# Linear attention, 32 heads: the outputs of two neighbouring heads stored by one transfer of 1 MB, and the orders drawn anew

## The chip, the cores and the metric

The kernel runs on one core of a Trainium2 chip. The core has five engines, each with its own in-order list of instructions: TensorE (PE, matmuls and transposes), VectorE (DVE), ScalarE (ACT), GpSimd (POOL) and SyncE (SP, which here only issues DMA transfers). Sixteen DMA engines move the bytes between HBM and the on-chip memory. The metric is the time of one execution in microseconds (us), the median of several runs. A profile shows one execution; its span, from the first to the last instruction, is a little shorter than that execution's time.

## The reference

Batch 1, 32 heads, 2048 positions, head size 128, all in bf16. One head is independent of the others.

```python
B, H, S, D = 1, 32, 2048, 128
phi_q = jnp.where(q > 0, q + 1, jnp.exp(q)) + 1e-6
phi_k = jnp.where(k > 0, k + 1, jnp.exp(k)) + 1e-6
kv = jnp.einsum("bhsd,bhse->bhde", phi_k, v)
z = jnp.einsum("bhsd->bhd", phi_k)
num = jnp.einsum("bhqd,bhde->bhqe", phi_q, kv)
den = jnp.einsum("bhqd,bhd->bhq", phi_q, z)[..., None] + 1e-6
return num / den
```

## The kernel before

**Tiling.** A head's q, k, v and output are 512 KB each. A head lies on the chip as 128 partitions with 16 rows of 128 numbers each (4 KB a partition, `rows`, 16 tiles j). Since max(x, 0) + min(exp(x), 1) is phi without the 1e-6, a head needs two parts of k and two of q: `em` (exp by ACT at L416, then min with 1 and plus 1e-6 by DVE at L392) and `rk` (max with 0, by POOL at L399 or DVE at L398).

**The operations of head h**, by the keys that the orders use:

- `ldk`, `ldv`, `ldq` (L388): loads. q of heads 2 to 29 and k and v of heads 8 to 29 come in pairs of heads, 1 MB each; the others are 512 KB. Each has six slots (`NI`), so a load waits until the users of the head six earlier are done.
- `ek` (L416, ACT), `em` (L392, DVE), `rk` (POOL or DVE, by the table `ON`), `v1` (L429, POOL or DVE): k's two parts, and v copied beside a column of ones, so that the same matmul gives z.
- `kv` (L437, PE): 32 matmuls, accumulated; `kvs` (L403, DVE) copies the result to SBUF. `kv` of the next head waits for it.
- `T` (L455, PE): 16 transposes of q in two halves into one PSUM tile, which must be free of the previous head's `eq`, `rqa` and `rqb`.
- `eq` (L467, ACT), `emq` (L392, DVE), `rqa` (L397, ACT, the first `NA[h]` of 16 tiles) and `rqb` (L398, DVE, the rest): q's two parts.
- `n` (L498, L503, L505, PE): 32 matmuls a head that give numerator and denominator, in two groups (three for head 31), each into PSUM banks that the previous head's division must have left.
- `a`, `r` (L522, L525, DVE), `f` (L529, DVE): 1e-6 added, the reciprocal, and the division into the output tile `o_sb`.
- `st` (L538, SP): the store. `o_sb` has 14 slots (`NO`), so the `f` of head h waits for the store of head h - 14. Heads 2, 3 and 31 are stored in three pieces, some of them for 51, 64, 13, 68 or 60 partitions (`ROWS`, `HALF`); all others with one transfer of 512 KB.
- `w0` to `w9` (L368, PE): 21 warm-up matmuls that use no data.
- `ident`, `ones`, `eps`, `v1ones` (constants), and `exp` (L361), a first activation on `ones` that makes ACT load its table.

**Order.** The table `ORDER` lists, by hand, the keys of each engine in the sequence in which it runs them. `Program.resolve` gives every operation the semaphore waits that its inputs and its slots need; an engine that waits holds up all that stands behind it in its list. SP issues all transfers on one queue, but ldv0.0, which ACT issues on its own (`BY_ACT`); this one load also waits for `ident`.

The loads and stores near each other in SP's list, one line as an example:

```python
        ldv28.0 st11.0 st12.0 ldk30.0 st14.0 ldk31.0 st13.0 ldq30.0 st19.0 ldv30.0 st18.0 st21.0 ldq31.0
```

The start of ACT's list:

```python
        ldv0.0 exp ek0.0 ek0.1 eq0.1 eq0.0 ek1.0 eq1.0 ek2.0 ek3.0 rqa2 eq2.0 ek4.0 eq3.0 rqa3 eq4.0 ek5.0
```

Of the kernel before, what the change touches and what calls it, by code (L numbers as in the profile page):

```python
# [107 lines left out]

ORDER = {
    "PE": """  # L110
        w9 w6 w8 w3 T0.1 T0.0 w1 kv0.0 T1.1 T1.0 kv0.1 w4 w2 kv1.0 w5 w7 w0 T2.1 T2.0 n0.0 kv2.0 n0.1 T3.0
        T3.1 n1.0 n1.1 kv3.0 T4.0 T4.1 n2.0 n2.1 T5.1 T5.0 kv4.0 n3.0 T6.0 T6.1 n3.1 kv5.0 n4.0 T7.1 T7.0
        n4.1 kv6.0 n5.0 T8.0 T8.1 n5.1 kv7.0 n6.0 T9.0 T9.1 kv8.0 n6.1 n7.0 T10.0 T10.1 n7.1 kv9.0 n8.0
        T11.0 n8.1 T11.1 kv10.0 n9.0 T12.0 T12.1 n9.1 kv11.0 n10.0 T13.0 T13.1 n10.1 kv12.0 n11.0 T14.0
        T14.1 n11.1 kv13.0 n12.0 T15.0 T15.1 n12.1 kv14.0 n13.0 T16.0 T16.1 n13.1 kv15.0 n14.0 T17.0 T17.1
        n14.1 kv16.0 n15.0 T18.0 T18.1 n15.1 kv17.0 n16.0 T19.0 T19.1 n16.1 kv18.0 n17.0 T20.0 T20.1 n17.1
        kv19.0 n18.0 T21.1 T21.0 n18.1 kv20.0 n19.0 T22.1 T22.0 n19.1 kv21.0 n20.0 T23.1 T23.0 kv22.0 n20.1
        n21.0 T24.1 T24.0 n21.1 kv23.0 n22.0 T25.1 T25.0 n22.1 kv24.0 n23.0 T26.0 T26.1 n23.1 kv25.0 n24.0
        T27.0 T27.1 n24.1 kv26.0 n25.0 T28.1 T28.0 n25.1 kv27.0 n26.0 T29.0 T29.1 n26.1 kv28.0 n27.0 T30.0
        kv29.0 n27.1 T30.1 n28.0 n28.1 kv30.0 n29.0 T31.0 n29.1 T31.1 kv31.0 n30.0 n30.1 n31.0 n31.1 n31.2  # L120
    """,
    "DVE": """
        ones v1ones0 eps0 rk0.0 v1ones1 em0.0 em0.1 rk0.1 emq0.1 rqb0.1 rqb0.0 v10.1 v11.0 eps1 rk1.0 em1.0
        kvs0 rk2.0 emq0.0 eps2 rqb1.0 rk3.0 emq1.0 kvs1 em2.0 v12.0 r0.0 f0.0 rqb2.0 a0.1 r0.1 kvs2 f0.1
        em3.0 emq2.0 r1.0 em4.0 rqb3.0 emq3.0 a1.1 f1.0 r1.1 f1.1 kvs3 rqb4.0 r2.0 f2.0 em5.0 emq4.0 a2.1
        kvs4 r2.1 rqb5.0 f2.1 r3.0 f3.0 emq5.0 em6.0 a3.1 r3.1 rqb6.0 f3.1 r4.0 kvs5 f4.0 emq6.0 em7.0 a4.1
        r4.1 rqb7.0 f4.1 r5.0 kvs6 f5.0 emq7.0 em8.0 a5.1 r5.1 rqb8.0 f5.1 r6.0 kvs7 f6.0 emq8.0 em9.0 a6.1
        rqb9.0 r6.1 f6.1 r7.0 kvs8 f7.0 emq9.0 em10.0 a7.1 kvs9 r7.1 rqb10.0 f7.1 r8.0 f8.0 emq10.0 em11.0
        a8.1 rqb11.0 r8.1 kvs10 f8.1 r9.0 f9.0 emq11.0 em12.0 a9.1 r9.1 rqb12.0 f9.1 r10.0 kvs11 f10.0
        emq12.0 em13.0 a10.1 r10.1 rqb13.0 f10.1 r11.0 kvs12 f11.0 emq13.0 em14.0 a11.1 r11.1 rqb14.0 f11.1  # L130
        r12.0 kvs13 f12.0 emq14.0 em15.0 a12.1 r12.1 rqb15.0 f12.1 r13.0 kvs14 f13.0 emq15.0 em16.0 a13.1
# [6 lines left out]
        kvs25 r23.1 rqb26.0 f23.1 r24.0 f24.0 em27.0 emq26.0 a24.1 kvs26 r24.1 rqb27.0 f24.1 r25.0 f25.0  # L138
        emq27.0 em28.0 a25.1 kvs27 r25.1 rqb28.0 f25.1 r26.0 f26.0 em29.0 emq28.0 a26.1 r26.1 kvs28 f26.1
        rqb29.0 r27.0 emq29.0 f27.0 a27.1 r27.1 kvs29 f27.1 em30.0 r28.0 f28.0 a28.1 r28.1 kvs30 f28.1  # L140
        em31.0 r29.0 f29.0 emq30.0 emq31.0 kvs31 a29.1 emq31.1 r29.1 emq31.2 f29.1 r30.0 f30.0 a30.1 r30.1
        f30.1 r31.0 f31.0 a31.1 r31.2 r31.1 f31.2 f31.1
    """,
    "ACT": """
        ldv0.0 exp ek0.0 ek0.1 eq0.1 eq0.0 ek1.0 eq1.0 ek2.0 ek3.0 rqa2 eq2.0 ek4.0 eq3.0 rqa3 eq4.0 ek5.0
        eq5.0 rqa5 ek6.0 eq6.0 rqa6 ek7.0 eq7.0 rqa7 ek8.0 eq8.0 rqa8 ek9.0 eq9.0 rqa9 ek10.0 eq10.0 rqa10
# [8 lines left out]
        rk10.0 v110.0 v111.0 rk11.0 v112.0 rk12.0 v113.0 rk13.0 v114.0 rk14.0 v115.0 rk15.0 v116.0 rk16.0
        rk17.0 v117.0 rk18.0 v118.0 v119.0 rk19.0 v120.0 rk20.0 rk21.0 v121.0 v122.0 rk22.0 rk23.0 v123.0
        rk24.0 v124.0 v125.0 rk25.0 v126.0 rk26.0 rk27.0 v127.0 v128.0 rk28.0 rk29.0 v129.0 rk30.0 v130.0
        rk31.0 v131.0
# [12 lines left out]

# [95 lines left out]
def bass_standalone__linear_attn_elu__prompt_kernel(nc: bass.Bass, q: bass.AP, k: bass.AP, v: bass.AP, out: bass.AP):  # L267
    B, H, S, D = q.shape
    assert D == P and S == 16 * P and B * H == NH
    NT = S // P  # L270
# [5 lines left out]
    qf, kf, vf, of = (t.rearrange("b h s d -> (b h) s d") for t in (q, k, v, out))  # L276
    rows = lambda t, h: t[h].rearrange("(p j) d -> p j d", j=NT)

    with ExitStack() as es:
# [85 lines left out]
        def warm(key, n):  # L365
            def g(e):
                for w in range(n):
                    ins = e.matmul(o_ps[:, 512:992], lhsT=ident[:], rhs=_ap(ident[:, :], 0, [[0, 4], [1, 120]]),  # L368
                                   start=(w == 0), stop=(w == n - 1))
# [215 lines left out]
```

## Time and profile before

| what | value |
|---|---|
| median of 3 runs | 167.99 us (167.9 to 168.12) |
| the profiled execution's own time | 167.83 us |
| its span | 166.5 us |
| PE busy | 156.6 us (94%), 2709 matmuls |
| DVE busy | 154.6 us (93%), 307 instructions |
| ACT busy | 146.6 us (88%) |
| POOL busy | 83.7 us (50%) |
| TensorE clock granted | 0.994 |
| HBM | 50.33 MB read, 16.78 MB written, 403 GB/s over the span |
| stores of 512 KB | 29, median 15.5 us from issue to landing |
| paired loads of 1 MB | q 14 (17.6 us), k 11 (16.4 us), v 11 (15.0 us) |

How to read it: the profile gives for each engine the time in which it ran instructions. Waiting and the issuing of DMA transfers aren't busy time. "q" behind an engine's name is its sequencer, which issues the transfers. A transfer's time to landing includes the wait behind the transfers that were issued earlier. The profile names tiles `la` throughout, so that instructions are told apart by line, shape and place in time; in each engine's list they run in the order of `ORDER`.

### The profile page before, as it was taken

The numbers are of one execution on the slowest core, as the hardware profiler recorded it, in microseconds if no ns is written. First come the engines' busy times: TensorE is split into PE (matmuls) and PEld (weight loads), VectorE is DVE, ScalarE is ACT, GpSimd is POOL, SyncE is SP. The second block draws the span as 40 slices with busy tenths as digits, with TensorE's granted clock in tenths as the row PEclk, the third lists the DMA queues.
The fourth block names the chain that finished last, engine by engine and source line by source line (L and its number), as shares of the span: only waits on it lengthen the run. The fifth ranks groups of instructions, "written<-read, shape, count | busy, mean of one in ns | idle before, by whom it ended". The sixth has DMA issues, their size and how long they took to land.

```text
span 166.5 us, 6111 instructions
## 1 busy us (share of the span) xinstructions
PE 156.6 (94%) x2709; PEld 150.9 (91%) x2709; DVE 154.6 (93%) x307; ACT 146.6 (88%) x99; POOL 83.7 (50%) x64
## 2 busy tenths in 40 slices
PE   4999997999999999999999999999999999999950
...
DVE  0498999999999999999999999999999999999992
...
DMA  5999999999999999999999999999999999999997
GB/s 224 410 424 411 422 403 418 403 405 404 420 418 412 414 406 427 411 423 410 417 408 423 415 424 404 420 415 424 407 416 422 413 416 414 416 416 413 385 396 279
DMA packets 16542, 67.51 MB, mean 405 GB/s; under 512 B 1539, under 2 KB 1923, under 8 KB 14723
## 3 DMA queue, kind: packets, MB, share of 16 engines
q1 hardware_dynamic: 16371, 66.59, 98.5%
q8 instruction: 21, 0.34, 0.8%
q10 hardware_dynamic: 144, 0.52, 0.8%
...
HBM read 50.33 MB, written 16.78 MB: 403 GB/s over the span
## 4 chain that ended last, share of the span: by engine, by line
PE 83%; DMA 7%; DVE 6%; SPq 2%; issue 0%
PE la L437 33%; PE la L503 18%; PE la L505 16%; PE la L455 16%; DMA la<-in_q_dram 7%; DVE la L529 4%; SPq L388 2%; DVE la L398 1%; DVE la L525 1%; PE la L498 0%; DVE la L522 0%; DVE la L403 0%
## 5 line engine op out<-in xcount | busy, mean ns | idle before, releaser
L529 DVE TENSOR_TENSOR la<-la 128x1536 bf16<-128x1536 f32 (+1 forms) x65 | 77.9, 1200 | 0.6
L503 PE MATMUL la<-la 128*128 128x129 bf16 x512 | 66.6, 219 | 0.1
L505 PE MATMUL la<-la 128*128 128x129 bf16 x512 | 66.6, 219 | 0.0
L399 POOL TENSOR_SCALAR la<-la 128x2048 bf16<-128x2048 bf16 x28 | 53.0, 1893 | 26.2 <-DVE la L522 18.7
L467 ACT ACTIVATE la<-la 128x2048 bf16<-128x2048 bf16 (+2 forms) x35 | 60.2, 1728 | 5.0 <-PE la L455 3.1
L416 ACT ACTIVATE la<-la 128x2048 bf16<-128x2048 bf16 (+1 forms) x33 | 61.3, 1865 | 3.4 <-DMA la<-in_k_dram 1.9
L437 PE MATMUL la<-la 128*128 128x129 bf16 x1024 | 63.4, 220 | 0.0
L437 PEld LDWEIGHTS la<-la 128*128 128x128 bf16 x1024 | 59.3, 98 | 0.8 <-DVE la L403 0.4
L429 POOL COPY la<-la 128x1024 int32<-128x1024 int32 (+1 forms) x30 | 31.2, 1043 | 41.1 <-PE la L437 22.7
L505 PEld LDWEIGHTS la<-la 128*128 128x128 bf16 x512 | 49.8, 97 | 0.0
L503 PEld LDWEIGHTS la<-la 128*128 128x128 bf16 x512 | 48.1, 97 | 0.3 <-DVE la L529 0.2
L392 DVE TENSOR_SCALAR la<-la 128x2048 bf16<-128x2048 bf16 (+2 forms) x68 | 42.4, 658 | 1.1 <-ACT la L416 1.1
L455 PE MATMUL la<-la 128*128 128x128 bf16 x512 | 35.3, 222 | 1.0 <-DMA la<-in_q_dram 0.9
L455 PEld LDWEIGHTS la<-la 128*128 128x128 bf16 x512 | 30.7, 99 | 2.7 <-DMA la<-in_q_dram 1.5
L397 ACT ACTIVATE la<-la 128x1024 bf16<-128x1024 bf16 (+2 forms) x29 | 31.6, 1091 | 0.0
L398 DVE TENSOR_SCALAR la<-la 128x1024 bf16<-128x1024 bf16 (+2 forms) x36 | 24.4, 682 | 4.7 <-DMA la<-in_k_dram 4.6
L498 PE MATMUL la<-la 128*128 128x3 bf16 (+1 forms) x128 | 21.6, 168 | 2.5 <-DVE la L529 2.5
L498 PEld LDWEIGHTS la<-la 128*128 128x128 bf16 x128 | 12.5, 98 | 2.8 <-DVE la L529 2.8
L525 DVE RECIPROCAL la<-la 128x12 f32<-128x12 f32 (+1 forms) x65 | 12.9, 200 | 1.0 <-PE la L505 0.2
L403 DVE CAST la<-la 128x129 bf16<-128x129 f32 x32 | 8.3, 258 | 0.0
L368 PE MATMUL la<-la 128*128 128x480 bf16 x21 | 6.7, 468 | 1.5 <-POOL la L353 1.5
L368 PEld LDWEIGHTS la<-la 128*128 128x128 bf16 x21 | 2.3, 120 | 3.9 <-issue 1.7
(15 smaller groups left out, 9.7 us busy)
## 6 DMA issues: line engine op xcount, KB each, us to landing
out_dram<-la SPq DMA_DIRECT2D x29, 512.0 KB, 15.5
la<-in_q_dram SPq DMA_DIRECT2D x14, 1024.0 KB, 17.6
la<-in_v_dram SPq DMA_DIRECT2D x11, 1024.0 KB, 15.0
la<-in_k_dram SPq DMA_DIRECT2D x11, 1024.0 KB, 16.4
...
```

The source lines that it names most:

```text
L392: add(on(key, "DVE"), key, lambda e: e.tensor_scalar(t, t, 1.0, EPS, op0=ALU.min, op1=ALU.add), deps)
L397: "ACT": lambda e: e.activation(dst, src, ACT.Relu),
L399: "POOL": lambda e: e.tensor_scalar(dst, src, BIG, 0.0, op0=ALU.min, op1=ALU.max)}[eng], deps)
L416: add("ACT", key, lambda e, a=a, b=b: e.activation(em_sb[:, h % NE, a:b], k_sb[:, h % NI["k"], a:b], ACT.Exp), [f"ldk{k0}.0"] + fill("em", ...
L429: add(on(key, "POOL"), key, lambda e, a=a, b=b, word=word: e.tensor_copy(v1_sb[:, h % NV, a:b, 0:D].bitcast(word), v_sb[:, h % NI["v"], a: ...
L437: ins = e.matmul(kv_ps, lhsT=src[:, j], rhs=v1_sb[:, h % NV, j, 0:NC], start=(j + part == 0), stop=(j == NT - 1 and part == 1))
L455: ins = e.transpose(to, src, ident[:])
L467: add("ACT", key, lambda e, a=a, b=b: e.activation(part(emq_sb, a, b), src(a, b), ACT.Exp), over("T", h, t_parts, a, b) + fill("emq", NQ, ...
L498: e.matmul(_ap(o_ps[:, :], o + D, [[NC, m]]), lhsT=ones[:], rhs=epsr[:, 0:m], start=True, stop=False, skip_group_check=True)
L503: e.matmul(to, lhsT=tile(emq_sb, t), rhs=kvs_sb[:, h % NK, 0:NC], start=late and c == 0, stop=False, skip_group_check=True)
L505: ins = e.matmul(to, lhsT=tile(rq_sb, t), rhs=kvs_sb[:, h % NK, 0:NC], start=False, stop=True, skip_group_check=True)
L529: return e.tensor_tensor(out=_ap(o_sb[:, :, :, :], first(o_sb[:, h % NO, t0, 0:1]) - first(o_sb[:, :, :, :]), [[m * D, nb], [D, m], [1, D] ...
```

## The change

The stores of heads 4 to 27 are joined in twelve pairs. One transfer of 1 MB moves both heads of a pair; each partition's 8 KB in `o_sb` go out as 4 KB of the first head and 4 KB of the second. It waits for both heads' divisions, has one semaphore, and frees both slots. Heads 0 to 3 and 28 to 31 are stored as before. SP's list has 85 transfers instead of 97.

All five lists of `ORDER` were drawn anew. Among what differs besides the stores' places:

- ACT runs `exp` before it issues `ldv0.0`, and `eq2.0` before `rqa2`.
- `v10.0` and `v13.0` move from POOL to DVE; `v10.1`, `rk0.0` and `rk2.0` from DVE to POOL. `v10.0` is DVE's third operation.
- PE's warm-up matmuls stand elsewhere; `w2` (4 matmuls) now comes between `kv1.0` and `T2`.
- ACT takes 14 instead of 8 tiles of q's relu in head 28 (`NA`).
- Many loads and stores have other places in SP's list.

```diff
-ON = {"rk0.1": "DVE", "v10.1": "DVE", "rk0.0": "DVE", "rk1.0": "DVE", "rk2.0": "DVE", "rk3.0": "DVE", "v12.0":
-      "DVE", "v11.0": "DVE"}
+ON = {"rk0.1": "DVE", "v11.0": "DVE", "rk1.0": "DVE", "rk3.0": "DVE", "v12.0": "DVE", "v10.0": "DVE", "v13.0":
+      "DVE"}
+SFIRST, SLAST = 4, 28
...
+def spair(h):
+    return SFIRST <= h < SLAST
...
-NA = (8, 0, 10, 8, 0, 8, 8, 8, 8, 8, 8, 8, 8, 8, 8, 8, 8, 8, 8, 8, 8, 8, 8, 8, 8, 8, 8, 8, 8, 8, 16, 16)
+NA = (8, 0, 10, 8, 0, 8, 8, 8, 8, 8, 8, 8, 8, 8, 8, 8, 8, 8, 8, 8, 8, 8, 8, 8, 8, 8, 8, 8, 14, 16, 16, 16)
...
     "PE": """
-        w9 w6 w8 w3 T0.1 T0.0 w1 kv0.0 T1.1 T1.0 kv0.1 w4 w2 kv1.0 w5 w7 w0 T2.1 T2.0 n0.0 kv2.0 n0.1 T3.0
-        T3.1 n1.0 n1.1 kv3.0 T4.0 T4.1 n2.0 n2.1 T5.1 T5.0 kv4.0 n3.0 T6.0 T6.1 n3.1 kv5.0 n4.0 T7.1 T7.0
+        w5 w8 w6 w7 T0.0 T0.1 w1 kv0.0 T1.0 T1.1 w3 w4 kv0.1 w9 w0 kv1.0 w2 T2.1 T2.0 n0.0 kv2.0 n0.1 T3.0
+        T3.1 n1.0 n1.1 kv3.0 T4.1 T4.0 n2.0 n2.1 T5.0 T5.1 kv4.0 n3.0 T6.1 T6.0 n3.1 kv5.0 n4.0 T7.1 T7.0
...
-        T27.0 T27.1 n24.1 kv26.0 n25.0 T28.1 T28.0 n25.1 kv27.0 n26.0 T29.0 T29.1 n26.1 kv28.0 n27.0 T30.0
-        kv29.0 n27.1 T30.1 n28.0 n28.1 kv30.0 n29.0 T31.0 n29.1 T31.1 kv31.0 n30.0 n30.1 n31.0 n31.1 n31.2
+        T27.0 T27.1 n24.1 kv26.0 n25.0 T28.0 T28.1 n25.1 kv27.0 n26.0 n26.1 T29.0 T29.1 kv28.0 n27.0 kv29.0
+        n27.1 T30.1 T30.0 n28.0 kv30.0 n28.1 n29.0 T31.0 T31.1 n29.1 kv31.0 n30.0 n30.1 n31.0 n31.1 n31.2
     "DVE": """
-        ones v1ones0 eps0 rk0.0 v1ones1 em0.0 em0.1 rk0.1 emq0.1 rqb0.1 rqb0.0 v10.1 v11.0 eps1 rk1.0 em1.0
-        kvs0 rk2.0 emq0.0 eps2 rqb1.0 rk3.0 emq1.0 kvs1 em2.0 v12.0 r0.0 f0.0 rqb2.0 a0.1 r0.1 kvs2 f0.1
-        em3.0 emq2.0 r1.0 em4.0 rqb3.0 emq3.0 a1.1 f1.0 r1.1 f1.1 kvs3 rqb4.0 r2.0 f2.0 em5.0 emq4.0 a2.1
+        ones eps0 v10.0 v1ones0 em0.1 em0.0 rk0.1 rqb0.0 rqb0.1 emq0.0 eps2 rk1.0 emq0.1 em1.0 v11.0 v1ones1
+        kvs0 rqb1.0 emq1.0 eps1 em2.0 kvs1 rk3.0 v12.0 em3.0 r0.0 f0.0 rqb2.0 kvs2 a0.1 r0.1 f0.1 v13.0
+        em4.0 emq2.0 r1.0 rqb3.0 emq3.0 a1.1 f1.0 r1.1 f1.1 kvs3 rqb4.0 r2.0 emq4.0 f2.0 em5.0 a2.1 kvs4
...
     "ACT": """
-        ldv0.0 exp ek0.0 ek0.1 eq0.1 eq0.0 ek1.0 eq1.0 ek2.0 ek3.0 rqa2 eq2.0 ek4.0 eq3.0 rqa3 eq4.0 ek5.0
+        exp ldv0.0 ek0.1 ek0.0 eq0.0 eq0.1 ek1.0 eq1.0 ek2.0 ek3.0 eq2.0 rqa2 ek4.0 eq3.0 rqa3 eq4.0 ek5.0
...
     "POOL": """
-        ident0 ident v10.0 v13.0 rk5.0 rk4.0 v14.0 v15.0 v16.0 rk6.0 rk7.0 v17.0 rk8.0 v18.0 v19.0 rk9.0
+        ident0 ident rk0.0 v10.1 rk2.0 rk4.0 rk5.0 v14.0 v15.0 v16.0 rk6.0 rk7.0 v17.0 rk8.0 v18.0 v19.0
...
     "SP": """
-        ldq0.0 ldk0.0 ldq1.0 ldk1.0 ldv1.0 ldk3.0 ldk2.0 ldq2.0 ldv2.0 ldk4.0 ldv3.0 ldk5.0 ldq4.0 ldv5.0
-        ldv4.0 ldv6.0 ldk6.0 ldq6.0 ldv8.0 ldk7.0 ldv7.0 ldk8.0 ldq8.0 st0.0 ldv10.0 st3.1 ldk10.0 ldq10.0
-        ldv12.0 ldk12.0 ldq12.0 ldv14.0 st1.0 st3.2 ldk14.0 ldq14.0 st2.2 ldv16.0 st2.1 ldk16.0 ldq16.0
-        st2.0 st4.0 ldv18.0 ldk18.0 ldq18.0 ldv20.0 st3.0 ldk20.0 ldq20.0 st5.0 st7.0 ldk22.0 ldq22.0
-        ldv22.0 st6.0 ldv24.0 ldq24.0 ldk24.0 st8.0 ldq26.0 st9.0 ldv26.0 ldk26.0 st10.0 ldk28.0 ldq28.0
-        ldv28.0 st11.0 st12.0 ldk30.0 st14.0 ldk31.0 st13.0 ldq30.0 st19.0 ldv30.0 st18.0 st21.0 ldq31.0
-        ldv31.0 st15.0 st24.0 st17.0 st16.0 st20.0 st25.0 st23.0 st22.0 st27.0 st28.0 st29.0 st26.0 st30.0
-        st31.0 st31.2 st31.1
+        ldq0.0 ldk0.0 ldq1.0 ldk1.0 ldv1.0 ldk2.0 ldk3.0 ldq2.0 ldv2.0 ldk4.0 ldv3.0 ldk5.0 ldq4.0 ldv4.0
+        ldv5.0 ldq6.0 ldv6.0 ldk6.0 ldv8.0 ldk7.0 ldv7.0 ldk8.0 ldq8.0 ldq10.0 ldk10.0 st2.1 ldv10.0 ldv12.0
+        ldq12.0 ldk12.0 ldq14.0 st3.0 ldk14.0 st1.0 st3.2 st0.0 ldv14.0 ldk16.0 st3.1 ldv16.0 ldq16.0
+        ldv18.0 ldq18.0 ldk18.0 st2.2 ldv20.0 ldq20.0 st2.0 st7.0 ldk20.0 st5.0 ldk22.0 ldv22.0 ldq22.0
+        ldv24.0 ldq24.0 ldk24.0 st9.0 ldq26.0 ldv26.0 ldk26.0 st11.0 ldv28.0 ldk28.0 ldq28.0 st13.0 ldq30.0
+        ldv31.0 ldk31.0 ldv30.0 ldk30.0 st15.0 st23.0 ldq31.0 st17.0 st19.0 st27.0 st21.0 st25.0 st29.0
+        st28.0 st30.0 st31.0 st31.2 st31.1
...
+            if spair(h):
+                if h % 2:
+                    key = f"st{h}.0"
+                    add("SP", key, lambda e: e.dma_start(of[h - 1:h + 1].rearrange("h (p j) d -> p h j d", j=NT),
+                                                         o_sb[:, (h - 1) % NO:(h - 1) % NO + 2]),
+                        [f"f{x}.{j}" for x in (h - 1, h) for j in range(len(groups(x)))], dma=f"o{(h - 1) % NO}")
+                    used("o", NO, (h - 1, h), key)
+                return
             for i, (a, b, x, y) in enumerate(st_parts(h)):
```

More of the change, by code (lines that the diff above doesn't have):

```diff
@@ L110 @@
     "PE": """
-        w9 w6 w8 w3 T0.1 T0.0 w1 kv0.0 T1.1 T1.0 kv0.1 w4 w2 kv1.0 w5 w7 w0 T2.1 T2.0 n0.0 kv2.0 n0.1 T3.0
-        T3.1 n1.0 n1.1 kv3.0 T4.0 T4.1 n2.0 n2.1 T5.1 T5.0 kv4.0 n3.0 T6.0 T6.1 n3.1 kv5.0 n4.0 T7.1 T7.0
-        n4.1 kv6.0 n5.0 T8.0 T8.1 n5.1 kv7.0 n6.0 T9.0 T9.1 kv8.0 n6.1 n7.0 T10.0 T10.1 n7.1 kv9.0 n8.0
-        T11.0 n8.1 T11.1 kv10.0 n9.0 T12.0 T12.1 n9.1 kv11.0 n10.0 T13.0 T13.1 n10.1 kv12.0 n11.0 T14.0
+        w5 w8 w6 w7 T0.0 T0.1 w1 kv0.0 T1.0 T1.1 w3 w4 kv0.1 w9 w0 kv1.0 w2 T2.1 T2.0 n0.0 kv2.0 n0.1 T3.0
+        T3.1 n1.0 n1.1 kv3.0 T4.1 T4.0 n2.0 n2.1 T5.0 T5.1 kv4.0 n3.0 T6.1 T6.0 n3.1 kv5.0 n4.0 T7.1 T7.0
+        n4.1 kv6.0 n5.0 T8.1 T8.0 n5.1 kv7.0 n6.0 T9.0 T9.1 n6.1 kv8.0 n7.0 T10.0 T10.1 n7.1 kv9.0 n8.0
+        T11.0 T11.1 n8.1 kv10.0 n9.0 T12.0 T12.1 n9.1 kv11.0 n10.0 T13.0 T13.1 n10.1 kv12.0 n11.0 T14.0
         T14.1 n11.1 kv13.0 n12.0 T15.0 T15.1 n12.1 kv14.0 n13.0 T16.0 T16.1 n13.1 kv15.0 n14.0 T17.0 T17.1
@@ L137 @@
         f21.1 r22.0 f22.0 em25.0 emq24.0 a22.1 rqb25.0 r22.1 f22.1 r23.0 kvs24 f23.0 emq25.0 em26.0 a23.1
[L138 to L142, printed above, removed]
+        kvs25 r23.1 rqb26.0 f23.1 r24.0 f24.0 emq26.0 em27.0 a24.1 rqb27.0 r24.1 kvs26 f24.1 r25.0 f25.0
+        emq27.0 em28.0 a25.1 r25.1 kvs27 f25.1 r26.0 rqb28.0 f26.0 emq28.0 em29.0 a26.1 kvs28 r26.1 f26.1
+        r27.0 f27.0 emq29.0 a27.1 kvs29 r27.1 f27.1 em30.0 r28.0 f28.0 a28.1 kvs30 r28.1 f28.1 emq30.0 r29.0
+        em31.0 f29.0 emq31.2 emq31.1 a29.1 emq31.0 r29.1 f29.1 kvs31 r30.0 f30.0 a30.1 r30.1 f30.1 r31.0
+        f31.0 a31.1 r31.2 r31.1 f31.2 f31.1
     """,
     "ACT": """
-        ldv0.0 exp ek0.0 ek0.1 eq0.1 eq0.0 ek1.0 eq1.0 ek2.0 ek3.0 rqa2 eq2.0 ek4.0 eq3.0 rqa3 eq4.0 ek5.0
+        exp ldv0.0 ek0.1 ek0.0 eq0.0 eq0.1 ek1.0 eq1.0 ek2.0 ek3.0 eq2.0 rqa2 ek4.0 eq3.0 rqa3 eq4.0 ek5.0
         eq5.0 rqa5 ek6.0 eq6.0 rqa6 ek7.0 eq7.0 rqa7 ek8.0 eq8.0 rqa8 ek9.0 eq9.0 rqa9 ek10.0 eq10.0 rqa10
@@ L149 @@
         ek21.0 eq21.0 rqa21 ek22.0 eq22.0 rqa22 ek23.0 eq23.0 rqa23 ek24.0 eq24.0 rqa24 ek25.0 eq25.0 rqa25
-        ek26.0 eq26.0 rqa26 ek27.0 eq27.0 rqa27 ek28.0 eq28.0 rqa28 ek29.0 eq29.0 rqa29 ek30.0 ek31.0 eq30.0
-        rqa30 eq31.0 eq31.2 eq31.1 rqa31
+        ek26.0 eq26.0 rqa26 ek27.0 eq27.0 rqa27 ek28.0 rqa28 eq28.0 ek29.0 eq29.0 rqa29 ek30.0 eq30.0 rqa30
+        ek31.0 eq31.0 eq31.1 eq31.2 rqa31
     """,
     "POOL": """
-        ident0 ident v10.0 v13.0 rk5.0 rk4.0 v14.0 v15.0 v16.0 rk6.0 rk7.0 v17.0 rk8.0 v18.0 v19.0 rk9.0
@@ L155 @@
[L155 to L158, printed above, removed]
+        ident0 ident rk0.0 v10.1 rk2.0 rk4.0 rk5.0 v14.0 v15.0 v16.0 rk6.0 rk7.0 v17.0 rk8.0 v18.0 v19.0
+        rk9.0 rk10.0 v110.0 v111.0 rk11.0 v112.0 rk12.0 v113.0 rk13.0 v114.0 rk14.0 v115.0 rk15.0 v116.0
```

9 lines of the change are left out of this document (6 added, 3 removed).

## The prediction

> **What bounds the kernel now.** I read the page's slices, then windows by engine, then the start of each engine's timeline, the chain of waits, the tail, and last the DMA issues one by one. First two rows of the slices and the DMA rows:
>
> ```profile
> PE   4999997999999999999999999999999999999950
> DVE  0498999999999999999999999999999999999992
> DMA  5999999999999999999999999999999999999997
> q1 hardware_dynamic: 16371, 66.59, 98.5%
> ```
>
> Three things are full at once. The windows of all engines say how full (columns: stretch, its length, then busy us of PE, PEld, DVE, ACT, POOL, clock, DMA share and GB/s):
>
> ```profile
> 60.00:90.00 30.00, 30.00 (x550) 30.00 (x548) 29.76 (x60) 29.62 (x20) 19.48 (x14) 1.00 1.02 415
> 156.00:158.00 2.00, 1.94 (x34) 1.63 (x31) 1.93 (x8) 0.99 (x1) 0.00 (x0) 1.00 0.84 342
> 158.00:164.00 6.00, 2.13 (x37) 1.92 (x36) 5.27 (x11) 0.00 (x0) 0.00 (x0) 1.00 0.98 394
> 164.00:166.50 2.50, 0.00 (x0) 0.00 (x0) 0.00 (x0) 0.00 (x0) 0.00 (x0) 0.64 0.57 213
> ```
>
> From 30 to 158 us PE never stops, one head each 4.62 us, and the DMA engines never stop either. So there are two ends: the chain of PE and DVE (last division f31.1 over at 163.38) and the DMA queue (last landing 166.48). The order of everything between decides neither as long as both stay fed. Only the start, where PE still idles, and the tail can move. The start is in the timelines (start, length, instruction, idle before it and its releaser):
>
> ```profile
> 1.50 0.41 ACTq L388 DMA_DIRECT2D la<-in_v_dram  x1
> 1.94 1.28 ACT L361 ACT_TABLE_LOAD   x1 [1.94 <-POOL la L353]
> 3.23 0.21 ACT L361 ACTIVATE la<-la 128x1 bf16<-128x1 bf16 x1
> ...
> 5.17 0.43 DVE L398 TENSOR_SCALAR la<-la 128x1024 bf16<-128x1024 bf16 x1 [4.12 <-DMA la<-in_k_dram]
> ...
> 7.11 0.61 POOL L429 COPY la<-la 128x512 int32<-128x512 int32 x1 [5.65 <-DMA la<-in_v_dram]
> ```
> ```profile
> 12.44 1.99 PE L437 MATMUL la<-la 128*128 128x129 bf16 x32
> 14.26 0.97 PE L368 MATMUL la<-la 128*128 128x480 bf16 x4
> 15.43 1.05 PE L455 MATMUL la<-la 128*128 128x128 bf16 x16 [0.19 <-DMA la<-in_q_dram]
> ```
>
> ldv0 is issued at 1.50, before the table load and exp, and lands at 7.06; POOL copies it while DVE already works from 5.17. PE has warm-up matmuls (L368) to spare until ldq2 lands at 15.29. Then the chain of waits has, in the window from 24 us:
>
> ```profile
> 25.15 1.66 DVE la L529
> ...
> 27.82 1.20 DVE la L398
> ...
> 29.07 1.07 PE la L455 x16
> ```
>
> f1.0 holds n2.0 (1.03 us of PE idle), then rqb4 holds T5 until 29.07. From T5 on PE runs without a gap, so whatever T5 loses, the compute end loses.
>
> **The change, part by part.** Base: span 166.5, profiled execution 167.83, that is 1.33 around the span; the median 167.99 is 0.16 above that execution.
>
> 1. *Twelve pair stores for 24 single ones.* Bytes, queue and packet size (4 KB) stay. Landings one after another price the two forms: the 13 half-megabyte transfers from the landing of st12 (135.26) to that of st24 (151.50) take 16.24, 1.249 each; the 10 stores from there to st26 (163.91) take 1.241 each. The trace has no paired store; the nearest rows are the paired k and v loads, the same pattern the other way: ldv8, ldk8, ldv12, ldk12 land 2.53, 2.55, 2.56, 2.54 after the one ahead, against 2 x 1.277 for single loads at 24 to 29 us. Bounds for the twelve: from 12 x (2.53 - 2.555) = -0.3 to +0.9, if a paired store moved at the single loads' 1.277 rather than 1.241 (24 halves x 0.036). I take 0, nearest to loads that show no difference. Each transfer also ends in a 4-byte packet of 9 ns on each DMA engine: -0.1. [...]
>
> By the Trainium skill, DMA: Bandwidth & Descriptors, section "Rules for kernel authors", a transfer should have 1 MiB or more, and its section "Anatomy of one DMA" gives 2.0 us fixed per transfer; twelve fewer would be 24 us less, 144. The landings 1.25 apart say that this part is hidden behind the next transfer, so the sum goes by the rows.
>
> 2. *The SP queue drawn anew.* Counted in half megabytes, I moved each load's measured landing by 1.26 per unit that its place moved and compared with its first use. All stay in time; the closest are ldv14 (6.0 later, 0.2 to spare), ldk30 (5.0 later, 0.3), ldq22 (3.0 later, 4.25 shrinks to 0.5), ldk20 (3.0 later, 0.7) and ldq28 (3.0 later, 0.9). Slots of o: st15 now frees slots 0 and 1 at about 145.3 for f28.0 at 149.29; the others have 3.7 or more. SP's longest block is at st27, for f27.1 at 148.3: what was queued before it lands until 152.9, 4.6 of cover, of which an issue needs about 1.0 (first packet 1.77 after an issue at 0.73). Behind it wait st21, st25, st29, st28, st30, st31, which hold up only the end itself. Cost 0; without that cover, the excess one to one.
>
> 3. *Start.* ACT issues ldv0 after exp. exp waits only for `ones` (over at 0.99); with 1.28 and 0.21 the issue comes at 2.48 rather than 1.50. At the measured 5.6 to landing it lands at L = 8.1; bounds 7.1 (if the engines reach it as soon as before) and 9.1 (one more queued transfer first). DVE now begins with v10.0, so DVE starts at L instead of 5.17, but gives rk0.0 (0.43), v10.1 (0.41) and rk2.0 (0.69) to POOL, which is idle until 20.5, and takes v10.0 (0.41) and v13.0 (0.69). Walked with the measured steps from one DVE instruction to the next: v10.0 0.38, em0.1 and em0.0 0.35 each, rk0.1 0.34, rqb0.0 and rqb0.1 0.60 each, emq0.0 0.38, rk1.0 0.60, emq0.1 0.34, em1.0 0.60, v11.0 0.62: kvs0 starts at L+5.2 and ends at L+5.5 (12.38 before). PE: kv1.0 at L+5.5, 1.82 long, then w2 with four warm-up matmuls (0.8): T2 at L+8.1 = 16.2 against 15.43. n0.0 then ends at L+10.6, f0.0 at L+12.65, rqb2.0 at L+13.15, so T3 at L+13.2 = 21.3 (20.16). ACT runs eq2.0 ahead of rqa2, then ek4.0, eq3.0, rqa3: eq4 ends at L+20.9, since T4 waits behind kv3.0 (over at L+17.85). rqb4.0 (1.23) follows, T5 at L+22.15 = 30.25: **+1.2** (bounds +0.4 at 7.1, where ldq2's landing binds, +2.2 at 9.1).
>
> 4. *Head 28.* ACT relu 14 tiles instead of 8: (1.237 - 1.025) / 2 = 0.106 a tile, +0.64, covered by ACT's gaps of 1.09 and 1.12 before ek31.0 and eq31.0; DVE -0.45, not on the path, since f30.0 waits for n30.0 (157.36). T29 stands behind n26.1 now (140.0 for 139.57), and rqb28, which now waits for rqa28 too, ends near 139.9. Cost 0; without those gaps 0.2 to 0.6.
>
> 5. *Tail.* The last store is issued when f31.1 ends. Before: 163.40, landed 166.48, 3.08 later. On an empty queue the first load took 2.70 to 3.19 from issue to its first and last landing, 1.27 of it data; with the store's 8 packets of 65 ns (0.52) that is 1.95 to 2.44. So 0.64 to 1.13 of compute delay hides behind the stores queued ahead; I take 0.8.
>
> **Sum:** 1.2 - 0.8 = +0.4 on the compute end; the DMA end alone would be -0.1. Span 166.9, median about 168.4.
>
> **Rivals.** *B, the cover is enough:* ldv0 lands near 7.1, T5 loses 0.4, and the queue alone sets the end: 167.99 - 0.1 = 167.9. For it: both ends are full and the bytes equal; before, ldv0's packets began only at 4.45, behind two loads, so a later issue may cost little. Against: DVE's first work hangs on ldv0 now. Decides if T5 is less than 0.6 to 1.1 late.
>
> *C, faster:* the seams between stores cost DMA time. With -0.3 and -0.1 from part 1 and B's start, 167.5. For it: single loads lost 0.02 per megabyte to paired ones. Against: stores already run at 1.241.
>
> *D, slower by loads:* the queue is late where slack shrank, above all ldq22, on which PE itself waits. Beyond 0.5 plus whatever PE is already late (so from about 1.7 at +1.2) each us is a us. A queue 2.5 late gives +0.8 on A: 169.2. For it: the landings drift by 3 us against a straight line over the run, since some DMA engines run behind others, by up to 4.8. Against: the measured landings already hold that lag.
>
> *E, paired stores are slow:* the halves of a partition's 8 KB lie 512 KB apart in HBM, so the writes lose what part 1's upper bound says, all on the DMA end: +0.9 - 0.1 = 168.8. Against: paired loads with that distance show nothing. The Trainium skill, DMA: Bandwidth & Descriptors, "Latency and other measured facts", has copies with a pitch of 512 KiB between partitions at 207 GB/s against 214; that is the rule that speaks against the change, no row here shows it for writes, and 3% of the paired stores' 30 us would be 1.0.
>
> That the store isn't what it says (fewer engines, smaller packets) has under 1 in 100: the paired loads do it.
>
> **Chances.** A 0.38, B 0.25, C 0.17, D 0.14, E 0.06. A change within 0.2% (0.34 us) can't be told from none here. A's own range is 168.1 to 169.0; 0.10 of it lies under 168.33, 0.28 above; 0.04 of B lies below 167.65. Faster 0.17 + 0.04 = 0.21, same 0.10 + 0.21 = 0.31, slower 0.28 + 0.14 + 0.06 = 0.48. The range: C with some margin at 167.3, D and the upper bound of part 3 (+2.2 - 0.8) at 169.5.
>
> **What would show it.** ldv0's issue near 2.5 and DVE's first copy near 8.1; T2 near 16.2, T5 near 30.2, n30.0 over near 158.5; no PE gap after T5; twelve 1 MB stores landing 2.5 after the one ahead; DMA share 1.02 to 158. T5 before 29.5 makes B or C right; a PE gap at L455 after 30 us, D; stores 2.55 or more apart, E.

## The result and the profile after

| | before | after |
|---|---|---|
| median of 10 runs each | 168.00 us (167.75 to 168.15) | 168.71 us (168.18 to 170.11) |
| ratio, 95% interval | | 1.0045 [1.0028, 1.0062] |
| the profiled execution's own time | 167.83 | 168.68 |
| its span | 166.5 | 167.4 |
| T2, T3, T5 start | 15.43, 20.16, 29.07 | 16.43, 21.05, 29.99 |
| n30.0 over, f31.1 over | 157.36, 163.38 | 158.36, 164.38 |
| last four landings | 166.42, 166.45, 166.46, 166.48 | 166.45, 166.51, 166.60, 167.34 |

The changed kernel is 0.45% slower, 0.7 us. Starts, ends and landings are read from the trace of one execution each. "n30.0 over" is the end of head 30's first group of `n`, "f31.1 over" that of the last division; a store lands sixteen times, once on each DMA engine, and the last four of these landings are given. The rows of the page after that answer to those of before, slices and DMA queues (packets, MB, share of 16 engines):

```profile
PE   4989997999999999999999999999999999999950
DVE  0199899999999999999999999999999999999992
DMA  5999999999999999999999999999999999999995
q1 hardware_dynamic: 16179, 66.59, 98.0%
q8 instruction: 21, 0.34, 0.8%
...
q14 instruction: 6, 0.05, 0.1%
...
out_dram<-la SPq DMA_DIRECT2D x12, 1024.0 KB, 17.2
```

The bytes are the same, twelve stores carry 1 MB. The `instruction` rows count the packets that bring the engines their instructions. They stand on the page of before too; the prediction passed them over. Windows of all engines after (columns as before):

```profile
60.00:90.00 30.00, 30.00 (x550) 30.00 (x548) 29.76 (x61) 29.48 (x21) 19.10 (x13) 1.00 1.02 414
156.00:158.00 2.00, 2.00 (x41) 2.00 (x39) 1.84 (x7) 2.00 (x2) 0.00 (x0) 1.00 1.00 408
158.00:164.00 6.00, 3.08 (x50) 2.55 (x48) 5.86 (x14) 0.00 (x0) 0.00 (x0) 1.00 0.96 386
164.00:166.50 2.50, 0.00 (x0) 0.00 (x0) 0.38 (x1) 0.00 (x0) 0.00 (x0) 0.66 0.66 243
```

In the middle nothing changed: PE full, DMA share 1.02. From 158 to 164 PE has 3.08 us of work left where it had 2.13: compute comes about 1 us later into the tail. Where it lost that is seen in the timelines of ACT, DVE (one row) and PE (start, length, instruction, idle before it):

```profile
0.73 1.28 ACT L365 ACT_TABLE_LOAD   x1 [0.73 <-PEq L582]
1.50 0.41 ACTq L392 DMA_DIRECT2D la<-in_v_dram  x1
2.03 0.20 ACT L365 ACTIVATE la<-la 128x1 bf16<-128x1 bf16 x1
```
```profile
7.77 0.43 DVE L433 COPY la<-la 128x1024 bf16<-128x1024 bf16 x1 [6.75 <-DMA la<-in_v_dram]
```
```profile
13.79 1.99 PE L441 MATMUL la<-la 128*128 128x129 bf16 x32 [0.39 <-DVE la L407]
15.62 0.97 PE L372 MATMUL la<-la 128*128 128x480 bf16 x4
16.43 1.06 PE L459 MATMUL la<-la 128*128 128x128 bf16 x16
```

ldv0 is issued at 1.50 as before, not at 2.5: the table load starts at 0.73, and the issue goes out beside it, ahead of the ACTIVATE that stands in front of it in the list. DVE waits 6.75 us for this load, which lands at 7.74 (7.06 before, from the same issue), and then everything follows from it: kv1 at 13.79, the four warm-up matmuls of `w2`, T2 at 16.43. The chain of waits, window from 24 us:

```profile
26.07 1.67 DVE la L533
...
28.75 1.20 DVE la L402
...
29.99 1.01 PE la L459 x15
```

The same three links as before (f1.0, rqb4, T5), 0.92 later. From there PE has no gap of its own but those of the tail, which were there before, so f31.1 is 1.00 later. Yet all landings but one are over at 166.60, 0.12 later than before. That one comes alone at 167.34, and it ends the run.

### The profile page after: what moved, and what is told of

Its sections match the earlier page's. It is cut to its first block, busy times and chain, and to the rows that moved or that the text cites. A ratio compares the mean times of both kernels' runs of the same rounds, so it can differ in the third digit from the quotient of the medians.

```text
span 167.4 us, 6085 instructions
## 1 busy us (share of the span) xinstructions
PE 156.5 (94%) x2709; PEld 150.9 (90%) x2709; DVE 153.6 (92%) x305; ACT 148.1 (88%) x99; POOL 86.3 (52%) x65
## 4 chain that ended last, share of the span: by engine, by line
PE 83%; DVE 10%; DMA 4%; ACT 0%; issue 0%
PE la L441 34%; PE la L507 17%; PE la L509 16%; PE la L459 16%; DVE la L533 5%; DMA la<-in_v_dram 4%; DVE la L402 2%; DVE la L396 2%; DVE la L433 1%; DVE la L529 1%; PE la L372 0%; ACT L365 0%; DVE la L407 0%; PE la L502 0%; DVE la L526 0%
## 5 line engine op out<-in xcount | busy, mean ns | idle before, releaser
L403 POOL TENSOR_SCALAR la<-la 128x2048 bf16<-128x2048 bf16 (+1 forms) x30 | 56.4, 1879 | 38.3 <-DVE la L526 16.8
L441 PEld LDWEIGHTS la<-la 128*128 128x128 bf16 x1024 | 59.3, 98 | 2.4 <-DVE la L396 1.3
L509 PEld LDWEIGHTS la<-la 128*128 128x128 bf16 x512 | 49.8, 97 | 0.0
L507 PEld LDWEIGHTS la<-la 128*128 128x128 bf16 x512 | 48.1, 97 | 0.4 <-DVE la L407 0.3
L433 POOL COPY la<-la 128x1024 int32<-128x1024 int32 (+1 forms) x29 | 30.4, 1051 | 27.2 <-PE la L441 25.7
L401 ACT ACTIVATE la<-la 128x1024 bf16<-128x1024 bf16 (+3 forms) x29 | 33.2, 1144 | 0.2 <-PE la L509 0.2
L459 PEld LDWEIGHTS la<-la 128*128 128x128 bf16 x512 | 30.6, 99 | 2.2 <-DMA la<-in_q_dram 1.5
L402 DVE TENSOR_SCALAR la<-la 128x1024 bf16<-128x1024 bf16 (+3 forms) x33 | 22.2, 678 | 0.0
L502 PEld LDWEIGHTS la<-la 128*128 128x128 bf16 x128 | 12.5, 98 | 2.7 <-DVE la L533 2.7
L433 DVE COPY la<-la 128x2048 bf16<-128x2048 bf16 (+1 forms) x4 | 2.5, 622 | 6.8 <-DMA la<-in_v_dram 6.8
```

The costliest lines, as they stand in the source:

```text
L401: "ACT": lambda e: e.activation(dst, src, ACT.Relu),
L403: "POOL": lambda e: e.tensor_scalar(dst, src, BIG, 0.0, op0=ALU.min, op1=ALU.max)}[eng], deps)
L433: add(on(key, "POOL"), key, lambda e, a=a, b=b, word=word: e.tensor_copy(v1_sb[:, h % NV, a:b, 0:D].bitcast(word), v_sb[:, h % NI["v"], a: ...
L441: ins = e.matmul(kv_ps, lhsT=src[:, j], rhs=v1_sb[:, h % NV, j, 0:NC], start=(j + part == 0), stop=(j == NT - 1 and part == 1))
L459: ins = e.transpose(to, src, ident[:])
L502: e.matmul(_ap(o_ps[:, :], o + D, [[NC, m]]), lhsT=ones[:], rhs=epsr[:, 0:m], start=True, stop=False, skip_group_check=True)
```

## The experiments

All ratios are against the kernel before, run on the same chip among the others. Three groups were run; in them the kernel before had medians of 168.13 (35 runs), 168.19 (27) and 168.14 (34). "f31.1" is the end of the last division, "others" the last landing but one, "packet" the start of the last 8 KB `instruction` packet, all from the one execution that was profiled, which need not be the median one: that of `pairs` is its longest of eleven (168.33), that of `early` its longest of twelve (169.32), that of `single` one of its long ones (168.86).

| kernel | ratio [95%] | T5 | f31.1 | others | last landing | packet |
|---|---|---|---|---|---|---|
| before | | 29.07 | 163.38 | 166.46 | 166.48 | 160.9 |
| after | 1.0045 [1.0028, 1.0062] | 29.99 | 164.38 | 166.60 | 167.34 | 165.9 |
| pairs | 0.9997 [0.9988, 1.0007] | 30.44 | 164.72 | 166.69 | 166.91 | 162.0 |
| newstart | 0.9998 [0.9989, 1.0007] | 29.91 | 164.17 | 166.65 | 166.66 | 160.8 |
| single | 1.0018 [1.0000, 1.0036] | 30.50 | 165.08 | 167.06 | 167.52 | 164.4 |
| oldstart | 1.0026 [1.0010, 1.0042] | 30.24 | 164.65 | 166.81 | 166.87 | 162.4 |
| oldstart_sp | 0.9999 [0.9990, 1.0007] | 29.43 | 164.20 | 166.77 | 166.85 | 162.3 |
| less_before | 0.9938 [0.9925, 0.9950] | 29.60 | 163.89 | 165.86 | 165.87 | 160.4 |
| less_after | 1.0022 [1.0013, 1.0031] | 29.87 | 164.24 | 166.21 | 167.17 | 165.8 |
| pad | 1.0035 [1.0018, 1.0051] | 29.63 | 164.00 | 166.94 | 167.14 | 165.8 |
| dvepad | 1.0022 [1.0005, 1.0038] | 29.79 | 164.20 | 166.79 | 166.98 | 162.1 |
| tail | 1.0033 [1.0023, 1.0044] | 29.98 | 164.38 | 166.93 | 167.30 | 166.0 |
| early | 1.0012 [1.0000, 1.0023] | 30.66 | 165.05 | 167.02 | 167.98 | 166.6 |
| both | 1.0012 [0.9999, 1.0024] | 29.68 | 164.09 | 166.79 | 166.84 | 162.0 |

**The pair stores alone** (`pairs`): the kernel before, with the paired store and each pair at a place near those of its two singles.

```diff
+SFIRST, SLAST = 4, 28
...
-        ldv28.0 st11.0 st12.0 ldk30.0 st14.0 ldk31.0 st13.0 ldq30.0 st19.0 ldv30.0 st18.0 st21.0 ldq31.0
...
+        ldk24.0 ldq26.0 st9.0 ldv26.0 ldk26.0 ldk28.0 st11.0 ldq28.0 ldv28.0 st13.0 ldk30.0 st15.0 ldk31.0
+        ldq30.0 ldv30.0 st19.0 st21.0 ldq31.0 ldv31.0 st17.0 st25.0 st23.0 st27.0 st28.0 st29.0 st30.0 st31.0
```

> The kernel before with nothing changed but the stores of heads 4 to 27, joined in twelve pairs, each at a place in SP's list where its slots are freed in time and no load comes more than two half megabytes later. Theory S: the pairs cost nothing, 167.8 to 168.2, twelve landings 2.5 us after the one ahead. Rival P: 168.5 to 168.9, steps over 2.55. Rival F: depends on where the instruction packets of SP's shorter list fall; 168.5 if one falls after 164 us, else 168.0.

168.03 against 168.13: no difference. The other way round (`single`), the changed kernel with its pairs taken apart at the same places:

```diff
-SFIRST, SLAST = 4, 28
+SFIRST, SLAST = 32, 32
...
-        ldv31.0 ldk31.0 ldv30.0 ldk30.0 st15.0 st23.0 ldq31.0 st17.0 st19.0 st27.0 st21.0 st25.0 st29.0
...
+        ldq30.0 ldv31.0 ldk31.0 ldv30.0 ldk30.0 st14.0 st15.0 st22.0 st23.0 ldq31.0 st16.0 st17.0 st18.0 st19.0
+        st26.0 st27.0 st20.0 st21.0 st24.0 st25.0 st29.0 st28.0 st30.0 st31.0 st31.2 st31.1
```

> The changed kernel with each paired store split into two single ones at the same place; all orders kept. Theory S: stays at 168.6 to 168.8, T5 near 30.0. Rival P (pairing itself costs): 168.0 to 168.2. Rival F: SP's list is as long as before's again, so its last instruction packet falls earlier, and the time is 168.0 to 168.3 although T5 stays at 30.0.

168.36: 1.0018, with an interval that begins at 1.0000, so slower than before by little or nothing, and if anything less slow than the changed kernel; the intervals overlap. `pairs` is the clear one of the two: pairing brings nothing and of itself costs nothing.

**The start alone** (`newstart`, the kernel before with the changed start) and the reverse (`oldstart`, the changed kernel with the old start):

`newstart` takes `ON` and the beginnings of the five lists from the changed kernel (PE to n3.0, DVE to kvs4, ACT to ek5.0, POOL to v14.0, SP to ldk5.0), `oldstart` takes the same from the kernel before. ACT's first line of the two:

```python
        exp ldv0.0 ek0.1 ek0.0 eq0.0 eq0.1 ek1.0 eq1.0 ek2.0 ek3.0 eq2.0 rqa2 ek4.0 eq3.0 rqa3 eq4.0 ek5.0 eq5.0
        ...
        ldv0.0 exp ek0.0 ek0.1 eq0.1 eq0.0 ek1.0 eq1.0 ek2.0 ek3.0 rqa2 eq2.0 ek4.0 eq3.0 rqa3 eq4.0 ek5.0 eq5.0
```

> The kernel before with the changed start alone: ON and the lists of all engines up to head 4 as changed; single stores and before's order after that. Theory S (the start costs the difference of the changed kernel and oldstart, 0.19%): 168.3 to 168.6, T2 at 16.1 or later in its profile. Rival B (the DMA queue alone sets the end, so the start is free): 168.0 to 168.2.

> The changed kernel with the start of before: the table ON of before and the lists of PE, DVE, ACT, POOL and SP in before's order up to head 4, all later orders and the paired stores kept. Theory S (the start sets the end: T5 0.92 us later, f31.1 1.0 later): T5 back at 29.1, f31.1 back at about 163.4, median 168.0 to 168.2, 0.0 to +0.1% against before. Rival P (the paired stores or the new queue order cost): stays at 168.6 to 168.9. Rival F (the 8 KB instruction packet at 165.92 on one DMA engine makes most of the loss, since SP's list is the same as in the changed kernel): 168.4 to 168.7, with one landing 0.5 or more behind the rest.

`newstart` loses what was forecast for the compute and ends at the same time: T5 at 29.91, f31.1 0.79 later, 168.10 against 168.19. Its windows:

```profile
158.00:164.00 6.00, 2.87 (x47) 2.37 (x44) 5.83 (x13) 0.00 (x0) 0.00 (x0) 1.00 0.97 388
164.00:166.50 2.50, 0.00 (x0) 0.00 (x0) 0.17 (x1) 0.00 (x0) 0.00 (x0) 1.00 0.65 245
```

PE has 2.87 us left after 158 (2.13 before), but the DMA share is 0.97 and 0.65 (0.98 and 0.57 before): the queue still sets the end. `oldstart`, with the start taken back, stays slow at 168.58. So the start alone doesn't make a kernel slow, and taking it back doesn't make the changed one fast.

One thing came out otherwise than expected: in the profile of `oldstart` T5 isn't back at 29.1 but at 30.24, later than in the changed kernel, and in `pairs`, also with the old start, it is at 30.44. There DVE's third copy of v, v12.0, waits for its load, and PE's `kv2` behind it (first row `oldstart`, second `pairs`):

```profile
18.30 0.69 DVE L431 COPY la<-la 128x2048 bf16<-128x2048 bf16 x1 [0.88 <-DMA la<-in_v_dram]
```
```profile
18.51 0.69 DVE L431 COPY la<-la 128x2048 bf16<-128x2048 bf16 x1 [0.99 <-DMA la<-in_v_dram]
```

In `before`, `less_before` and `oldstart_sp` it doesn't wait. So T5 varies by more than the two starts differ: 29.07 to 30.44 in the five traces with the old start (mean 29.76), 29.63 to 30.66 in the nine with the new one (mean 30.00). The 0.92 between the two first traces is a difference of two executions, and the one before is the earliest of all fourteen.

**How large the cover is** (`less_before` and `less_after`). The cover is the delay of the compute end that the end of the DMA queue hides. Both kernels have 1 MB less in the queue: the first leaves the outputs of heads 20 and 22 unwritten, the second those of heads 20 and 21. The edit of the first:

```diff
+LEFT = (20, 22)
...
+                if h in LEFT:
+                    continue
```

> The kernel before without the stores of heads 20 and 22, so 1 MB less to write near the end; those two heads of the output are not written, all else is computed. Theory of the cover (the DMA queue sets before's end, 0.64 to 1.13 us behind what the last store alone would need): 0.5 to 1.1 us less, 167.0 to 167.6. Rival (the compute end sets it already): no change, 168.0 to 168.2.

> The changed kernel without the paired store of heads 20 and 21, 1 MB less to write near the end; those two heads are not written. Theory S (in the changed kernel the compute end sets the time, the cover is used up): at most 0.3 less, 168.4 to 168.7. Rival Q (the queue, late through its new order, sets it): 0.5 or more less, under 168.2.

The kernel before then takes 167.12, 1.07 less. Its windows:

```profile
158.00:164.00 6.00, 2.65 (x44) 2.30 (x44) 5.75 (x12) 0.00 (x0) 0.00 (x0) 1.00 0.81 322
164.00:166.50 2.50, 0.00 (x0) 0.00 (x0) 0.00 (x0) 0.00 (x0) 0.00 (x0) 0.83 0.32 120
```

The queue has room now (0.81 from 158 to 164), and the end is the compute's: the last store is issued at 163.91 and has landed at 165.87, 1.96 later. Held against before, where issue to landing took 3.08, the cover is 1.1. In `less_after` the other landings also come 1.94 after the issue (164.27, 166.21), but a lone one at 167.17 ends it: there 1 MB less brings only 0.2% (1.0022 for the changed kernel's 1.0045).

**The lone landing.** In the DMA view of `early` from 166.6 to 168.0 (slices, then packets and share by queue) the whole of the last traffic is:

```profile
DMA  5000000001000000000000000000000000000000
...
DMA packets 3, 0.01 MB, mean 7 GB/s; under 512 B 1, under 2 KB 2, under 8 KB 2
...
q14 instruction: 1, 0.01, 1.4%
q1 hardware_dynamic: 2, 0.00, 0.3%
```

In order of time these are one 8 KB instruction packet at 166.63 (309 ns), the last 1536 bytes of a store at 166.94, and its 4-byte packet at 167.00. All others had landed by 167.02, that one lands at 167.98. The trace doesn't name the DMA engine; that it is one and the same is read from the times, the packet ending as the 1536 bytes begin. In the changed kernel the packet starts at 165.92 (438 ns) and the last 4 bytes move at 166.41, for the landing at 167.34. Before, the last such packet starts at 160.9, among other traffic. Two kernels are to move it, by waits that are fulfilled already and only make a list longer. `pad` puts 16 into SP's list ahead of each of st1.0 and st29.0 (the stores on `o1`; two waits make one instruction, so the trace has 16 instructions more, 8 near 50 us and 8 near 151), `dvepad` 12 into DVE's, ahead of v10.0 (6 instructions more); the edits of `pad` and of `dvepad`:

```diff
+PAD = 16
...
+            if eng == "SP" and name == "o1":
+                for _ in range(PAD):
+                    engine.wait_ge(self.get("DVE"), 1)
```
```diff
+PAD = 12
...
+            if eng == "DVE" and fn is self.op["v10.0"][1]:
+                for _ in range(PAD):
+                    engine.wait_ge(self.get("POOL"), 1)
```

> The changed kernel with 16 more waits on SP behind the store of head 1, on a semaphore that has long been reached, so that they wait for nothing and only make SP's list longer. Theory S: 168.6 to 168.8, nothing changes. Rival F (SP fetches instructions as its list advances, and the last fetch now falls at 165.92 behind the last data of one DMA engine): the fetch moves to before 163, the last landing is with the rest, 168.0 to 168.3.

> The changed kernel with 12 more waits on DVE ahead of v10.0, where DVE idles until 7.7 us; they are on a semaphore that has long been reached, so that they only make DVE's list longer, 330 instructions instead of 318 (before has 328). Theory D (the packet of 8 KB at 165.9 is DVE's next piece of instructions, due near the end of its list, and falls behind the last data because the change shortened the list): the packet moves to between 157 and 163, no landing stands 0.5 or more behind the rest, and the time falls by 0.2 to 0.5, to 168.2 to 168.5. Rival (the packet isn't DVE's, as it wasn't SP's in the run pad): stays at 165.8, 168.7.

With SP's list longer, the last packet stays at 165.8 (an earlier one moves from 128.4 to 113.2). With DVE's list longer it is at 162.1, and the last landing stands 0.19 behind the others instead of 0.74, as in `pairs` (0.21); the DMA view from 165.9 to 167.0 has no instruction packet any more:

```profile
DMA packets 66, 0.08 MB, mean 76 GB/s; under 512 B 10, under 2 KB 66, under 8 KB 66
...
q1 hardware_dynamic: 66, 0.08, 20.7%
```

So the length of DVE's list moves it. With the separate waits counted, the trace has 328 DVE instructions before and 318 after, 325 in `single` and 324 in `dvepad`: the pairs need fewer waits. Length is not all, though: `oldstart` has 320 and its packet at 162.4, `single` 325 and 164.4.

How much the packet costs a trace shows by two distances. The first is from an engine's last 4 bytes to its landing (the sixteen of each taken in order of time): 0.32 to 0.47 in the kernels whose packet comes by 164.4, for all engines, but 0.93 to 0.98 for the lone one of `after`, `less_after` and `early`. In `single` the last landing stands out by 0.46 without that: its last 4 bytes move at 167.11 and are reported 0.41 later, so it is late with its data. The second is from the end of f31.1. Where nothing else holds it, the last store lands 1.96 to 1.99 after that (`less_before`, `less_after` and `early` but for the lone one); the lone landing comes 2.92 to 2.97 after it in `after`, `less_after`, `early` and `tail`, whose packet starts 1.54 to 1.58 after it (`pad` 1.79 and 3.14). So in these executions the run ends with the compute again, some 1.0 later than the last store needs, and the cover of 1.1 is nearly used up. For the changed kernel +1.00 at f31.1, -1.12 of cover and +0.98 make +0.86, and that is what its span is longer.

`dvepad` stands at 1.0022 where `pad` has 1.0035 and `tail` 1.0033: in the direction expected, but the intervals overlap.

**SP's order.** `oldstart_sp` is `oldstart` with the SP list of `pairs`; `early` is the changed kernel with that list up to st13, `tail` has only the last stores in another order, `both` is `tail` with the DVE waits. Of SP's list, the start of the difference of the first two and the whole one of the last two:

```diff
-        ldv5.0 ldq6.0 ldv6.0 ldk6.0 ldv8.0 ldk7.0 ldv7.0 ldk8.0 ldq8.0 ldq10.0 ldk10.0 st2.1 ldv10.0 ldv12.0
-        ldq12.0 ldk12.0 ldq14.0 st3.0 ldk14.0 st1.0 st3.2 st0.0 ldv14.0 ldk16.0 st3.1 ldv16.0 ldq16.0
...
+        ldv6.0 ldk6.0 ldq6.0 ldv8.0 ldk7.0 ldv7.0 ldk8.0 ldq8.0 st0.0 ldv10.0 st3.1 ldk10.0 ldq10.0 ldv12.0
+        ldk12.0 ldq12.0 ldv14.0 st1.0 st3.2 ldk14.0 ldq14.0 st2.2 ldv16.0 st2.1 ldk16.0 ldq16.0 st2.0 ldv18.0
```
```diff
-        ldv31.0 ldk31.0 ldv30.0 ldk30.0 st15.0 st23.0 ldq31.0 st17.0 st19.0 st27.0 st21.0 st25.0 st29.0
-        st28.0 st30.0 st31.0 st31.2 st31.1
...
+        ldk30.0 st15.0 st23.0 ldq31.0 st17.0 st19.0 st21.0 st25.0 st27.0 st28.0 st29.0 st30.0 st31.0 st31.2
+        st31.1
```

> The run oldstart (168.58) with one more part undone: SP's list of the run pairs (before's order with the pairs joined, 168.03) in place of the changed kernel's; PE, DVE, ACT and POOL keep the changed orders after head 4, and ACT its 14 tiles in head 28. Theory Q (the changed SP list holds the remaining 0.26%): 168.0 to 168.2. Rival O (the changed orders of the other engines hold it): 168.5 to 168.7.

> The changed kernel with SP's list up to st13 from the run pairs (before's order), and the changed list from ldq30 on. Theory Q-early (loads of the changed list, just in time, come late in some executions and stop PE): 168.2 to 168.4, and no run above 168.8. Rival Q-tail: 168.6 to 168.8.

> The changed kernel with another order at the end of SP's list: st21 and st25 ahead of st27, and st28 ahead of st29, so that no ready store stands behind one that waits. Theory Q-tail (with the changed list some executions run the queue dry at the end, the ones 0.5 above the others in oldstart and single): 168.2 to 168.5, and no run above 168.8. Rival (the loss comes from earlier in the list, or from the end of the compute): 168.6 to 168.8 with the same spread.

> The run dvepad and the run tail together. If both theories hold, 168.0 to 168.2, as before; if only D holds, as dvepad; if neither, 168.7.

`oldstart_sp` against `oldstart` is the clearest pair of the study: only SP's list differs, and the ratio goes from 1.0026 [1.0010, 1.0042] to 0.9999 [0.9990, 1.0007], though in two groups and on two chips. `early` falls to 1.0012, and its lone landing was seen in its longest execution alone; `tail` stays at 1.0033. That points to the first part of the list, up to st13, and not to the last stores. What the new order does there no profile shows: after T5 PE has the same gaps in all these kernels, and the last store of a whole head ahead of st30 lands between 163.9 and 164.5 in all that leave nothing unwritten. The times of `oldstart` lie in two groups, five from 168.13 to 168.39 and seven from 168.50 to 169.01; its profile is of the first group. Those of `single` do too (seven to 168.41, five from 168.74), and its profile is of the second: there ldv0 lands at 8.25, T5 is at 30.50, and f31.1 is 1.71 later than before, beyond the cover, so that the last store lands late (167.06, 1.95 after its issue). So a late start can make a long execution; whether it makes the second group of `oldstart` isn't shown, since no trace of that group is there.

`both` has 1.0012 [0.9999, 1.0024] and is not faster than before. Nor is `pairs`: no kernel here beats the one before.

## Why the prediction came out as it did

The forecast was 168.4 in 167.3 to 169.5, slower the likeliest. 168.71 lies in the range, on the right side, 0.3 above. But the sum that gave the 0.4 was not what made it slow: its start would have been hidden, and two things that it put at nothing or didn't have made up for that. So the number came near by luck in part.

1. **Pair stores, cost 0:** right. They land 2.5 apart (st27, st21, st25 at 156.51, 159.00, 161.51), and alone they give 0.9997. Rival C (-0.4, which from 167.99 gives 167.6 and not its 167.5) and rival E (+0.8) fall with it: the interval of `pairs` reaches from -0.2 to +0.12 us. The 2.0 us a transfer, which the prediction takes from the Trainium skill, DMA: Bandwidth & Descriptors, "Anatomy of one DMA", are given there for transfers that GpSimd issues; here SP issues them. The Trainium skill, DMA: Bandwidth & Descriptors, "Latency and other measured facts", has copies at a pitch of 512 KiB a little slower (207 GB/s for 214); for 4 KB pieces lying 512 KB apart within a store this kernel shows nothing of it.

2. **SP's queue, cost 0:** this is the step that failed. What was checked was whether each load comes before its first use, with landings moved by 1.26 per place. That held in the profiles; but the new list against the old one costs 0.27% in `oldstart`, 0.4 to 0.5 us, with no stall to show for it. Rival D put a price on late loads after T5; its sign, a gap at the transposes after 30 us, isn't there.

3. **Start, +1.2 at T5:** the chain was right, its first link wrong. The issue of ldv0 does not wait for exp; what delayed DVE is that its first copy now hangs on a load that lands near 7.7 instead of starting at 5.17 on another. The forecast gave T5 = L + 22.15; measured are 29.99 - 7.74 = 22.25. With L at 7.74 for 8.1, T5 came at +0.92 instead of +1.2, below the middle of the bounds; against the mean of the traces with the old start it is about +0.2. The prediction took both starts as fixed, but L lies between 7.37 and 8.40 in the nine traces with the new start, all with the issue at 1.50. How firmly the run hangs on it shows in `early`, whose profiled execution was the longest of its twelve (169.32; median 168.34):

```profile
8.42 0.43 DVE L431 COPY la<-la 128x1024 bf16<-128x1024 bf16 x1 [7.41 <-DMA la<-in_v_dram]
```

L is 0.65 later than in the changed kernel, f31.1 0.67 later (165.05 for 164.38), and the lone landing 0.63 later.

4. **Head 28, cost 0:** right as far as the trace tells. n30.0 is over at 158.36, 1.00 later, and T5 already 0.92 of it.

5. **Cover, 0.64 to 1.13, 0.8 taken:** mis-sized; it is 1.07 by the times and 1.1 by the trace. With 0.92 in point 3 the sum is no longer +0.4 but -0.2, hidden. `newstart` is that sum by itself, and gives nothing. Rival B was right about the start, though by its sign (T5 before 29.5) it should not have been: the cover was as large as its upper bound.

What stood in no case is the lone landing. The last 8 KB of instructions, sent at 160.9 before, now meet the last bytes of the last store, and the last landing comes 0.74 (`after`), 0.96 (`early`, `less_after`) or 0.38 us (`tail`) after all others. The packet itself takes only 0.31 to 0.44 of that; the last 4 bytes behind it are reported 0.93 to 0.98 later instead of 0.32 to 0.47. With it the compute end sets the end of the run after all, by a path that the sum didn't have. In `pad`, with the packet at 165.8, the last landing stands out by 0.20 only, no more than in `pairs` and `dvepad` without it; there the others land late too (166.94).

The ratios are consistent with two parts, about 0.24% for SP's list (`oldstart` 1.0026, `dvepad` 1.0022) and about 0.12% for the packet (`early` 1.0012), against 1.0033 to 1.0045 for both together. That they add up so is an inference from overlapping intervals, not shown; and `both`, which keeps the first part of the new list, has 1.0012 where this reading would have some 1.002.

**Open:** how SP's new order costs time; why DVE's list sets the place of that packet (the trace doesn't say whose instructions it carries); why the landing behind it lags by more than the packet's own time; how often in ten executions the packet falls there; and how much the start, which varies from one execution to the next, adds to the spread.
